# 384-column copies of the first batch and pair 4's casts moved to VectorE, the gate half decoded later

## The chip, the cores and the metric

The kernel runs on one core of a Trainium2 chip. The metric is device time in microseconds for one execution of the whole program, as the median of several runs. TensorE is called PE here, VectorE DVE, ScalarE ACT, GpSimd POOL and SyncE SP, as in the profile.

## What is computed

The reference chains three blocks on inputs of four batches of 576 positions and eight heads of 64 columns:

```python
# attention, block-causal mask with blocks of 64
scores = (q @ k.T) / 8 ; scores = where(mask, scores, -1e9)
x = softmax(scores) @ v                      # [4, 576, 512] after joining the heads
# gated unit
h = relu(x @ w_in) ; u, v = h[..., :512], h[..., 512:]
v_n = (v - mean(v)) / sqrt(var(v) + 1e-6)
x = (u * (w_spatial @ v_n + b_spatial)) @ w_out
# feed-forward
xn = (x - mean(x)) / sqrt(var(x) + 1e-6) * g_ln
out = x + relu(xn @ w_ch1) @ w_ch2
```

All of it is float32. Where the values need more accuracy than one fast product gives, an operand is split into a high part (rounded to the fast format, fp32r) and a low part (the rest), and three products are summed (`mm3`, lines 106 to 108).

## The kernel before

The program has an attention stage, in which the first products of the gated unit are already mixed in, then the spatial products and w_out, then the feed-forward. The change concerns the attention stage.

**Units.** Two heads form a pair, four pairs make a batch, 16 pairs in all. Each pair has nine units (`UNITS`, line 231): first the 64 last query rows of both heads (the tail, c = 4), then blocks of 128 query rows, c = 3, 2, 1, 0 for head j = 0 and 1, which need 512, 384, 256 and 128 key columns. The loop over units `u` (line 533) is written in this order: `scores(u)` on PE into PSUM (tag `sc`, three banks); `softmax(u)`, which is a mask and row minimum on DVE (line 296), then the exponential on ACT (line 303); two units later `transposes(u - 2)`, which turns the weights on PE (line 353, tag `tr`, two banks) and copies them from PSUM to the tiles `pH` (c of 2 and more, the tail among them) and `pL` (c of 0 and 1). At fixed units of the next pair follow `weighted`, the product with v (line 404, `pH` as part 1 and `pL` as part 0), `reciprocals` of the row sums (line 310: DVE, a transpose on PE into a `tr` bank, a copy `rr` on ACT, and two trips through HBM) and `store_x` (line 411, on POOL: the product with the reciprocals at line 414, the high part of `xT` at line 60, its low part at line 417).

**Who copies.** In `put` (line 342) a copy goes to DVE (line 345) if c is at least `PLAN["ev0"]` in the first batch, `PLAN["ev1"]` in the others, and else to ACT (line 347). Before, `ev0` is 3 and `ev1` is 2.

**Preparing a pair.** `prepare(p)` (line 198) is stepped one piece a unit while pair p - 1 is scored. Pairs 0 to 3 are packed (`PACKED` is 4): one cast of the queries and keys to the high part (`cp("hi", ...)`), and the low parts on POOL (line 209). From pair 4 on each head has its own half: two casts, and two subtractions on POOL for each (lines 221 and 223). `cp` picks the engine by `PLAN['hi0']` for pairs below 4 (`v`, DVE, line 56) and `PLAN['hi1']` from 4 on (`s`, ACT, line 58). The operand tiles are two, `stack0` and `stack1`, for even and odd pairs.

**Decoding w_in.** The weights come as 64-bit floats and are decoded on the chip by `decode` (line 81): an activation on ACT (line 88), a shift (line 89) and a shift-and-or (line 90) on DVE; `split` then puts the high part (line 101) and the low part (line 102) of `win` on POOL. There are eight pieces of 128x512, first four of the value half of w_in, then four of the gate half. The set `DECODE` (line 532) names the units at which `decode_in` is stepped: unit 1 starts the loads, the next four units decode the value half and the last four the gate half. Loads of later pieces are asked for as pieces are used. Unit 36 is the first of pair 4, unit 45 the first of pair 5.

**Mixed-in products.** From unit 44 on, `fill` hands out pieces of the value tiles (`vps`) and then of the gate units (`ups`), products of `xT` and `win`, between the units.

**What sets the order.** The program is written in this order, but a scheduler that goes by its own timeline puts each engine's instructions in a row of its own. A decode's ACT instruction (line 88) and its first DVE instruction (line 89) are pinned to the program's order (`here`). On an engine the instructions run in their row; across engines they wait for semaphores.

Of the kernel before, what the change touches and what calls it, by code (L numbers as in the profile page):

```python
# [17 lines left out]

PLAN = {'mm': 3, 'sc': 3, 'tr': 2, 'D': 2, 'hi0': 'v', 'hi1': 's', 'klo0': 'g', 'klo1': 'g', 'qlo0': 'g', 'qlo1': 'g', 'xm0': 'g', 'xm1': 'g', 'xh0': 'g', 'xh1': 'g', 'xl0': 'g', 'xl1': 'g', 'dm': 'g', 'dh': 'g', 'ev0': 3, 'ev1': 2, 'rate': 24500.0, 'vrb': 3, 'ds': 2, 'dy': 1, 'raw': 5, 'yn': 2, 'ts': 3, 'ring': 8, 'wt': 2, 'cb': 1, 'hq': 8, 'packed': 4, 'plain': 3, 'pre': 8, 'py': 10, 'pyn': 4, 'dn0': 2, 'dnn': 5, 'vl': 'v', 'pace': 3, 'wd': 7, 'tl0': 'v', 'tl1': 'v', 'xe': 's', 'pt': 6, 'dstart': 8}


def f32(ap):
    return ap.bitcast(F32)


def view(ap, offset, dims):

    return bass.AP(tensor=ap.tensor, offset=ap.offset + offset, ap=[list(ap.ap[0])] + [list(d) for d in dims])  # L30
# [3 lines left out]
def tile_kernel(  # L34
# [14 lines left out]
    def E(k, p=None):  # L49
        k = PLAN[k if p is None else k + ("0" if p < 4 else "1")]  # L50
        return {"v": nc.vector, "g": nc.gpsimd, "s": nc.scalar}[k]

    def cp(k, p, out, src):
        e = PLAN[k if p is None else k + ("0" if p < 4 else "1")]
        if e == "v":
            nc.vector.tensor_copy(out, src)
        elif e == "s":
            nc.scalar.copy(out, src)  # L58
        else:
            nc.gpsimd.tensor_scalar(out, src, 1.0, 0.0, op0=ALU.mult, op1=ALU.add)  # L60
# [66 lines left out]
    at = tc.alloc_tile_pool(name="at", bufs=2, side="right")  # L127
    p_mm = tc.alloc_tile_pool(name="p_mm", bufs=PLAN["mm"], space=PSUM, side="left")
    p_sc = tc.alloc_tile_pool(name="p_sc", bufs=PLAN["sc"], space=PSUM, side="right")
    p_tr = tc.alloc_tile_pool(name="p_tr", bufs=PLAN["tr"], space=PSUM, side="right")  # L130

# [4 lines left out]

    PACKED = PLAN['packed']
    nat = {}
# [31 lines left out]
    def clear(i):  # L170
        nc.gpsimd.memset(f32(qtail[i][:, 0]), 0.0)
        nc.gpsimd.memset(f32(qtail[i][:, 1]), 0.0)
# [25 lines left out]
    def prepare(p):  # L198

        raw, vt = nat.pop(p), vts.pop(p)  # L200
        st, qt = stacks[p % 2], qtail[p % 2]
        ops[p] = (st, qt, vt, raw)
        low, high = slice(0, 64), slice(64, 128)
        if p < PACKED:
            cp("hi", p, st[:, 0, 0:2, :], raw[:, 0])
            yield
            hi = f32(st[:, 0, 0:2, :])
            for i in range(2):
                E("klo",p).tensor_tensor(st[:, 1, i, :], raw[:, 0, i], hi[:, i], op=ALU.subtract)
            yield  # L210
            for j, rows in enumerate((low, high)):
                nc.scalar.copy(qt[rows, :, 0, 64 * j:64 * j + 64], f32(st[rows, :, 0, 512:S]))
                yield
            return
        if p < PACKED + 2:
            clear(p % 2)
            nc.gpsimd.memset(f32(st[high, :, 0, :]), 0.0)
        for j in range(2):
            cp("hi", p, st[:, j, 1:3, :], raw[:, j])
            yield  # L220
            nc.gpsimd.tensor_tensor(st[low, j, 0, :], raw[low, j, 0, :], f32(st[low, j, 1, :]), op=ALU.subtract)  # L221
            yield
            nc.gpsimd.tensor_tensor(st[high, j, 2, :], raw[high, j, 1, :], f32(st[high, j, 2, :]), op=ALU.subtract)
            yield
        nc.scalar.copy(
            view(qt, 0, [[192, 2], [256, 2], [1, 64]]), f32(view(st, 512, [[3 * S, 2], [S, 2], [1, 64]]))
        )
        yield
# [296 lines left out]
    for _ in prepare(0):  # L525
        pass
# [2 lines left out]
    size = [200 + (S if c == 4 else 128 * (c + 1)) for _, c in UNITS]  # L529
    tot = float(sum(size) * NP)  # L530
    D = PLAN['D']
    DECODE = {1, 7, 12, 17, 22, 38, 42, 46, 50}
    for u in range(NS + 8):
        p, i = divmod(u, NU)
        if u < NS:
# [16 lines left out]
        if i == 0:  # L552
            for q in range(2, PACKED) if p == 0 else range(max(p + 2, PACKED), p + 3):
                load(q)
            load_v(p + 2)
            if p + 1 < NPAIR:
                preps[0] = prepare(p + 1)
        if 0 in preps and i >= 1:
            next(preps[0], None)
        if u in DECODE:  # L560
            next(dec, None)
# [597 lines left out]
```

## Time and profile before

| what | us |
|---|---|
| median of 3 runs | 806.71 |
| lowest and highest run | 805.53 and 810.85 |
| the profiled execution | 807.45 |
| its span, first to last instruction | 805.5 |

The times of the runs and the profiled execution are those of the whole execution; the span leaves out 1.95 us around the instructions. All times in views of the trace count from the start of the span. A row of a timeline gives the start, the length, the engine, the line, the operation, its output and input, how many instructions are merged in it, and in brackets the idle time before it with what ended that. A row of waits gives the engine and line that waited, what it waited for, the sum, the number of waits and the longest.

### The profile page before, as it was taken

What the parts mean: (1) busy time and instruction counts of PE and PEld (TensorE: products, weight loads), DVE (VectorE), ACT (ScalarE), POOL (GpSimd) and SP (SyncE); (2) the same over time, 40 slices, a digit from 0 to 9 for tenths busy, and PEclk for the clock granted to TensorE, in tenths of its full rate; (3) what the DMA queues carried; (4) which work ended last, traced back from release to release, by engine and by line L of the source; (5) the groups of instructions that cost most, each with busy time, mean ns of one, the idle gap of its engine ahead of it and who ended that gap; (6) DMA issues with size and microseconds to landing.
All of it is one profiled execution on the core that took longest, in us unless ns stands there. A gap on an engine that the chain in (4) does not pass through costs nothing.

```text
span 805.5 us, 13270 instructions
## 1 busy us (share of the span) xinstructions
PE 781.1 (97%) x4498; PEld 667.3 (83%) x4498; DVE 528.4 (66%) x1193; ACT 419.2 (52%) x1071; POOL 413.8 (51%) x417
## 2 busy tenths in 40 slices
PE   9998999999999999899999999999999999999997
PEld 4666788778878799888888888888899888888986
DVE  5777666674564377776677777897566578645534
ACT  5777676566755454555354554553345454433421
POOL 5598866654543343222275455455545455545431
PEclk9999999999999999999999999999999999999999
DMA  8966445545251579778520333204001003000002
GB/s 245 208 169 175 130 134 152 141 124 168 68 158 51 151 223 284 214 243 272 165 92 0 105 115 96 79 1 157 1 15 39 1 1 123 22 0 1 1 1 78
DMA packets 53687, 88.66 MB, mean 110 GB/s; under 512 B 6770, under 2 KB 17138, under 8 KB 53620
## 3 DMA queue, kind: packets, MB, share of 16 engines
q1 hardware_dynamic: 53620, 87.83, 36.7%
q8 instruction: 35, 0.57, 0.3%
q14 instruction: 32, 0.26, 0.1%
HBM read 68.85 MB, written 18.95 MB: 109 GB/s over the span
## 4 chain that ended last, share of the span: by engine, by line
PE 72%; DVE 11%; DMA 6%; issue 3%; ACT 3%; POOL 3%; SPq 0%; ACTq 0%; DVEq 0%; POOLq 0%
PE hps L938 21%; PE o L106 8%; PE o L108 8%; PE o L107 8%; PE pv L404 5%; PE tr L353 4%; DMA raw<-in_w_ch_dram 3%; PE sc L281 3%; PE ups L106 2%; PE sc L275 2%; DVE pH L345 2%; PE ups L108 2%; PE ups L107 2%; PE vps L108 1%; PE vps L106 1%
## 5 line engine op out<-in xcount | busy, mean ns | idle before, releaser
L102 POOL TENSOR_TENSOR a<-s,a 128x256 fp32r<-128x256 f32 x96 | 78.2, 818 | 92.4 <-ACT a L97 92.4
L107 PE MATMUL o<-w,h 128*128 128x512 f32 x288 | 112.9, 393 | 0.0
L106 PE MATMUL o<-w,h 128*128 128x512 f32 x288 | 107.8, 398 | 1.6 <-ACT h L930 1.6
L944 DVE TENSOR_TENSOR c<-hps,c 128x384 f32<-128x384 f32 x120 | 66.5, 554 | 54.1 <-PE hps L938 52.3
L108 PE MATMUL o<-w,h 128*128 128x512 f32 x288 | 97.7, 398 | 0.3
L303 ACT ACTIVATE p<-p,nm 128x512 f32<-128x512 f32 (+3 forms) x128 | 71.2, 557 | 34.1 <-DVE nm L296 31.0
L296 DVE CUSTOM_DVE_ANT_0 p<-sc,mask 128x512 f32<-128x512 f32 (+3 forms) x128 | 58.9, 479 | 41.7 <-PE sc L281 16.4
L102 POOL TENSOR_TENSOR a<-w,a 128x256 fp32r<-128x256 f32 x72 | 60.7, 846 | 44.9 <-ACT a L97 39.4
L97 ACT CAST a<-s 128x256 fp32r<-128x256 f32 x96 | 38.4, 404 | 83.6 <-PE hps L938 76.5
L345 DVE COPY pH<-tr 128x512 f32<-128x512 f32 (+1 forms) x88 | 49.7, 575 | 26.0 <-PE tr L353 25.3
L106 PEld LDWEIGHTS o<-w,h 128*128 128x128 f32 x288 | 53.7, 187 | 12.3 <-ACT h L930 2.9
L107 PEld LDWEIGHTS o<-w,h 128*128 128x128 f32 x288 | 54.1, 188 | 10.1
L108 PEld LDWEIGHTS o<-w,h 128*128 128x128 f32 x288 | 53.1, 188 | 9.3 <-DVE h L931 1.6
L353 PE MATMUL tr<-idn,p 128*128 128x128 f32 x320 | 56.1, 283 | 4.2 <-DVE pH L345 4.2
L788 POOL TENSOR_TENSOR gt<-gf,gt 128x576 fp32r<-128x576 f32 (+1 forms) x17 | 25.6, 1507 | 61.8 <-ACT gt L787 61.8
L117 POOL TENSOR_TENSOR rs<-rs,nhalf 128x1 f32<-128x1 f32 x36 | 23.0, 639 | 59.2 <-DVE rs L116 54.0
L353 PEld LDWEIGHTS tr<-idn,p 128*128 128x128 f32 x320 | 38.4, 142 | 14.8 <-DVE pH L345 6.7
L88 ACT ACTIVATE dm<-raw 128x256 f32<-128x256 f32 (+1 forms) x72 | 31.9, 462 | 29.9 <-DVE w L90 9.1
L221 POOL TENSOR_TENSOR stack<-qkt,stack 64x576 fp32r<-64x576 f32 x24 | 34.5, 1436 | 25.0 <-ACT stack L58 24.0
L931 DVE SCALAR_TENSOR_TENSOR h<-c,h 128x384 fp32r<-128x384 f32 x72 | 45.4, 650 | 1.5 <-ACT h L930 1.5
L281 PE MATMUL sc<-stack 128*128 128x512 f32 (+3 forms) x192 | 43.7, 341 | 0.8 <-DVE nm L296 0.4
L930 ACT ACTIVATE h<-c 128x384 fp32r<-128x384 f32 x72 | 35.3, 520 | 16.6 <-DVE c L944 16.2
(183 smaller groups left out, 2257.1 us busy)
## 6 DMA issues: line engine op xcount, KB each, us to landing
raw<-in_w_ch_dram SPq DMA_DIRECT2D x64, 256.0 KB
qkt<-in_qk_dram SPq DMA_DIRECT2D x112, 144.0 KB
vt<-in_v_dram SPq DMA_DIRECT2D x16, 320.0 KB
rb<-r_d SPq DMA_DIRECT2D x32, 144.0 KB
u_d<-ur SPq DMA_DIRECT2D x16, 288.0 KB
us<-u_d SPq DMA_DIRECT2D x16, 288.0 KB
y_d<-ys SPq DMA_DIRECT2D x18, 256.0 KB
yr<-y_d SPq DMA_DIRECT2D x18, 256.0 KB
```

The lines of the kernel that those rows point to most:

```text
L102: {"v": nc.vector, "g": nc.gpsimd}[low].tensor_tensor(lo, src, f32(hi), op=ALU.subtract)
L106: MM(out_ps, lhsT=a[0], rhs=b[0], start=first, stop=False)
L107: MM(out_ps, lhsT=a[0], rhs=b[1], start=False, stop=False)
L108: MM(out_ps, lhsT=a[1], rhs=b[0], start=False, stop=last)
L281: MM(s_ps[:, :nn], lhsT=st[:, j, i, q], rhs=st[:, j, 2, 0:nn], start=(i == 0), stop=(i == 1))
L296: nc.vector.tensor_tensor_reduce(pt[:, o:o + n], s_ps[:, :n], m, -0.125, 3e38, ALU.add, ALU.min, nm[:, i:i + 1])
L303: nc.scalar.activation(pt[:, :n], pt[:, :n], AF.Exp, bias=nm[:, 0:1], scale=-1.0, accum_out=sm[:, col:col + 1])
L345: nc.vector.tensor_copy(out, src)
L353: nc.tensor.transpose(tr[:, o:o + 128], pt[:, 128 * kc:128 * kc + 128], idn)
L931: nc.vector.scalar_tensor_tensor(t[:, 1], src, 0.0, f32(t[:, 0]), op0=ALU.max, op1=ALU.subtract)
L938: MM(ps, lhsT=a[x], rhs=b[y], start=not more and kc == 0 and k == 0, stop=kc == KD // 2 - 1 and k == 2, skip_group_check=True,)
L944: nc.vector.tensor_tensor(out, ps, x, op=ALU.add)
```

## The change

Three places change. `ev0` goes from 3 to 2, so in the first batch the copies with c = 2 (384 columns, two in a pair) move from ACT to DVE. In `prepare`, pair 4's two casts take the engine of the first four pairs, DVE, in place of ACT; later pairs stay on ACT. And the four gate pieces of w_in are decoded at units 42, 45, 48 and 51 in place of 38, 42, 46 and 50.

```diff
-PLAN = {..., 'ev0': 3, 'ev1': 2, ...}
+PLAN = {..., 'ev0': 2, 'ev1': 2, ...}
...
         for j in range(2):
-            cp("hi", p, st[:, j, 1:3, :], raw[:, j])
+            cp("hi", 0 if p == PACKED else p, st[:, j, 1:3, :], raw[:, j])
             yield
...
-    DECODE = {1, 7, 12, 17, 22, 38, 42, 46, 50}
+    DECODE = {1, 7, 12, 17, 22, 42, 45, 48, 51}
```

The scheduler then orders the front of the program anew. On DVE, at the end of pair 2's scoring (line 296 is a mask with its row minimum, `pH_551` are pair 2's weights, `tr_545` and `tr_553` its transposed tail), this stood before:

```order
L296 ISA p_607,nm_608<-sc_603,mask_104 128x256
L296 ISA nm_608 128x1
L90 SCALAR_TENSOR_TENSOR dm_477<-dm_477,de_478 128x512
L296 ISA p_623,nm_624<-sc_619,mask_104 128x256
L296 ISA nm_624 128x1
L345 COPY pH_551<-tr_545 128x4x2x64
L345 COPY pH_551<-tr_553 128x2x64
```

and this stands there now:

```order
L90 SCALAR_TENSOR_TENSOR dm_477<-dm_477,de_478 128x512
L296 ISA p_583,nm_584<-sc_579,mask_104 128x384
L296 ISA nm_584 128x1
L296 ISA p_607,nm_608<-sc_603,mask_104 128x256
L296 ISA nm_608 128x1
L56 CAST stack0_95<-qkt_514 128x1152 x2
L296 ISA p_623,nm_624<-sc_619,mask_104 128x256
L296 ISA nm_624 128x1
L345 COPY pH_551<-tr_545 128x4x2x64
L345 COPY pH_551<-tr_553 128x2x64
```

Pair 4's casts have come in between the two 256-column masks, and a decode instruction has moved two masks ahead.

On DVE, behind pair 4's tail (`pH_916` are pair 4's weights, `dm_927` is the first gate piece of w_in), the order before was:

```order
L345 COPY pH_916<-tr_910 128x4x2x64
L345 COPY pH_916<-tr_918 128x2x64
L89 TENSOR_SCALAR de_928<-raw_394 128x512
L90 SCALAR_TENSOR_TENSOR dm_927<-dm_927,de_928 128x512
L345 COPY pH_916<-tr_944 128x4x128
```

and it is now:

```order
L345 COPY pH_916<-tr_910 128x4x2x64
L345 COPY pH_916<-tr_918 128x2x64
L345 COPY pH_916<-tr_935 128x4x128
L296 ISA p_997,nm_998<-sc_994,mask_104 128x128
L296 ISA nm_998 128x1
```

The two decode instructions are gone from this place; the first gate piece is decoded behind the next pair's tail masks.

On ACT, a little earlier (`stack0_95` receives pair 6's casts, `rr_871` is pair 3's copy of reciprocals, `pL_736` pair 3's weights), the order before was:

```order
L303 ACTIVATE p_968,sm_848<-p_968,nm_969 128x256
L58 CAST stack0_95<-qkt_878 128x1152
L318 COPY rr_871<-rps_869 9x128
L58 CAST stack0_95<-qkt_878 128x1152
L347 COPY pL_736<-tr_896 128x128
L303 ACTIVATE p_984,sm_848<-p_984,nm_985 128x256
L88 ACTIVATE dm_994<-raw_484 128x512
```

and it is now:

```order
L303 ACTIVATE p_959,sm_848<-p_959,nm_960 128x256
L58 CAST stack0_95<-qkt_878 128x1152 x2
L318 COPY rr_871<-rps_869 9x128
L347 COPY pL_736<-tr_896 128x128
L303 ACTIVATE p_975,sm_848<-p_975,nm_976 128x256
L88 ACTIVATE dm_985<-raw_394 128x512
L58 COPY xx_822<-pv_921 128x256
```

The copy of the reciprocals has moved behind the second cast, and one decode activation fewer stands in this stretch.

## Rows read from the trace of the kernel before

**Rows 1.** The page: busy time of each engine and share of the span
```profile
PE 781.1 (97%) x4498; PEld 667.3 (83%) x4498; DVE 528.4 (66%) x1193; ACT 419.2 (52%) x1071; POOL 413.8 (51%) x417
```

**Rows 2.** Waits of PE from 0 to 60 us
```profile
PE tr L353 <- DVE pH L345: 1.5, 4, 0.4
```

**Rows 3.** Windows: length, busy of PE, PEld, DVE, ACT, POOL; granted clock, DMA
```profile
60.00:82.00 22.00, 18.75 (x121) 14.13 (x118) 15.02 (x44) 16.06 (x49) 18.92 (x16) 0.92 0.61 160
66.00:68.00 2.00, 1.45 (x10) 0.71 (x9) 1.53 (x3) 2.00 (x6) 1.93 (x2) 0.77 0.01 2
68.00:70.00 2.00, 2.00 (x13) 1.67 (x10) 1.87 (x2) 0.73 (x2) 1.85 (x3) 0.50 0.64 191
```

**Rows 4.** Waits of PE from 60 to 82 us
```profile
PE sc L260 <- DVE nm L296: 0.6, 1, 0.6
PE tr L353 <- DVE pH L345: 0.6, 1, 0.6
PE tr L353 <- ACT pL L347: 0.6, 1, 0.6
PE rps L316 <- ACT pL L347: 0.5, 1, 0.5
PE tr L353 <- ACT rr L318: 0.5, 1, 0.5
```

**Rows 5.** Timeline of PE, near 40, 67 and 80 us
```profile
39.78 0.87 PE L404 MATMUL pv<-pL,vt 128*64 128x256 f32 x8
40.59 1.09 PE L353 MATMUL tr<-idn,p 128*128 128x128 f32 x8
...
67.05 1.55 PE L404 MATMUL pv<-pL,vt 128*64 128x256 f32 x8
68.53 1.97 PE L353 MATMUL tr<-idn,p 128*128 128x128 f32 x8
71.11 0.55 PE L353 MATMUL tr<-idn,p 128*128 128x128 f32 x3 [0.60 <-DVE pH L345]
...
80.57 0.50 PE L108 MATMUL vps<-win,xT 128*128 128x512 f32 x1 [0.21 <-POOL xT L417]
```

**Rows 6.** Timeline of DVE, 67 to 71 us
```profile
67.37 1.27 DVE L89 TENSOR_SCALAR de<-raw 128x512 uint32<-128x512 uint32 x1
68.77 1.68 DVE L90 SCALAR_TENSOR_TENSOR dm<-dm,de 128x512 uint32<-128x512 uint32 x1
70.37 0.68 DVE L345 COPY pH<-tr 128x512 f32<-128x512 f32 x1
```

**Rows 7.** Timeline of ACT, 60 to 67 us
```profile
60.94 0.65 ACT L88 ACTIVATE dm<-raw 128x512 f32<-128x512 f32 x1
...
65.28 0.24 ACT L318 COPY rr<-rps 9x128 f32<-9x128 f32 x1
65.44 1.15 ACT L58 CAST stack<-qkt 128x1152 fp32r<-128x1152 f32 x1
66.49 0.25 ACT L347 COPY pL<-tr 128x128 f32<-128x128 f32 x1
```

**Rows 8.** Groups by line and form, 0 to 200 us: busy, mean ns
```profile
L58 ACT CAST stack<-qkt 128x1152 fp32r<-128x1152 f32 x20 | 22.4, 1142 | 0.0
...
L345 DVE COPY pH<-tr 128x384 f32<-128x384 f32 x16 | 8.7, 547 | 0.1
...
L347 ACT COPY pH<-tr 128x384 f32<-128x384 f32 x8 | 3.7, 465 | 0.0
...
L56 DVE CAST stack<-qkt 128x1152 fp32r<-128x1152 f32 x4 | 3.0, 758 | 4.9 <-DMA qkt<-in_qk_dram 4.3 <-issue 0.5
```

**Rows 9.** Timeline of DVE, 39 to 46 us
```profile
39.38 0.89 DVE L345 COPY pH<-tr 128x512 f32<-128x512 f32 x2 [0.31 <-PE tr L353]
...
45.44 1.36 DVE L300 TENSOR_TENSOR nm<-nm 128x1 f32<-128x1 f32 x1
```

**Rows 10.** Timeline of POOL near 41 us
```profile
40.76 1.28 POOL L102 TENSOR_TENSOR win<-dm,win 128x512 fp32r<-128x512 f32 x1
```

More of the change, by code (lines that the diff above doesn't have):

```diff
@@ L17 @@
 DRAM = bass.MemoryType.DRAM
-PLAN = {'mm': 3, 'sc': 3, 'tr': 2, 'D': 2, 'hi0': 'v', 'hi1': 's', 'klo0': 'g', 'klo1': 'g', 'qlo0': 'g', 'qlo1': 'g', 'xm0': 'g', 'xm1': 'g', 'xh0': 'g', 'xh1': 'g', 'xl0': 'g', 'xl1': 'g', 'dm': 'g', 'dh': 'g', 'ev0': 3, 'ev1': 2, 'rate': 24500.0, 'vrb': 3, 'ds': 2, 'dy': 1, 'raw': 5, 'yn': 2, 'ts': 3, 'ring': 8, 'wt': 2, 'cb': 1, 'hq': 8, 'packed': 4, 'plain': 3, 'pre': 8, 'py': 10, 'pyn': 4, 'dn0': 2, 'dnn': 5, 'vl': 'v', 'pace': 3, 'wd': 7, 'tl0': 'v', 'tl1': 'v', 'xe': 's', 'pt': 6, 'dstart': 8}
+PLAN = {'mm': 3, 'sc': 3, 'tr': 2, 'D': 2, 'hi0': 'v', 'hi1': 's', 'klo0': 'g', 'klo1': 'g', 'qlo0': 'g', 'qlo1': 'g', 'xm0': 'g', 'xm1': 'g', 'xh0': 'g', 'xh1': 'g', 'xl0': 'g', 'xl1': 'g', 'dm': 'g', 'dh': 'g', 'ev0': 2, 'ev1': 2, 'rate': 24500.0, 'vrb': 3, 'ds': 2, 'dy': 1, 'raw': 5, 'yn': 2, 'ts': 3, 'ring': 8, 'wt': 2, 'cb': 1, 'hq': 8, 'packed': 4, 'plain': 3, 'pre': 8, 'py': 10, 'pyn': 4, 'dn0': 2, 'dnn': 5, 'vl': 'v', 'pace': 3, 'wd': 7, 'tl0': 'v', 'tl1': 'v', 'xe': 's', 'pt': 6, 'dstart': 8}
 def f32(ap):
```

## The prediction

> **What bounds the kernel now.** I read the page first. TensorE (PE) is busy 97% of the span [rows 1], so nothing that an idle engine saves counts until PE is shown waiting for it. The diff touches only the attention stage of the first batch and the decoding of the gate half of w_in. Laid beside each other, the orders of the two kernels part at the first of the moved copies, some 17 us into the span, and run alike again by about 170 us. What stands behind that is passed through: a microsecond won or lost in front moves the end by a microsecond. So I split the front by windows and read PE's waits in it. Up to 60 us the largest wait of PE is 1.5 us in four pieces, for VectorE's (DVE's) copies of transposed tiles [rows 2]. From 60 to 82 us, while pairs 4 and 5 are scored, the mean granted clock is 0.92 [rows 3], and five waits there, for DVE and ScalarE (ACT), make 0.6 + 0.6 + 0.6 + 0.5 + 0.5 = 2.8 us [rows 4]. There the clock itself falls: 0.77 from 66 to 68 us and 0.50, the 1.2 GHz level, from 68 to 70 us [rows 3]. Before it fell PE was busy only 1.45 of 2 us in the first of these windows.
>
> What that costs is in PE's timeline: eight weighted-value matmuls take 0.87 us at 39.78 us and 1.55 us at 67.05 us; the eight transposes behind them 1.09 us at 40.59 us and 1.97 us at 68.53 us [rows 5]. The clock thus costs 0.68 + 0.88 = 1.56 us. Together with the waits, some 4.4 us lie loose between 60 and 82 us. That is the size of the prize; 1% of the kernel is 8.1 us, and a change of less than that is about what a measurement of this kernel can't tell from none.
>
> **The change part by part.** *The gate half's decode moves from units 38, 42, 46 and 50 to 42, 45, 48 and 51.* The work is the same, only later. The one at unit 38 is what matters. On DVE its two instructions stand right between the tail copies and the 512-column copies of pair 4, which PE's next transposes need. They took 1.27 us at 67.37 us and 1.68 us at 68.77 us, and the copy behind them began at 70.37 us [rows 6]; PE then waited 0.60 us for that copy at 71.11 us [rows 5]. In the changed order this place is empty of decoding. PE's eight transposes ended late themselves because of the clock, so the copy can't come more than these 0.6 us earlier to any use: I take 0.6 us (0 if the transposes are the later end, 0.6 at most).
>
> On ACT the same decode's activation (0.65 us at 60.94 us) goes from the front of a stretch without a gap [rows 7]. But the order changes there too: before, the reciprocals' copy at 65.28 us stood between the two casts of pair 6, and now it stands behind both. It frees the PSUM bank that PE's tail transposes wait for (the 0.5 us on `rr` in [rows 4]). So it comes 1.15 us later by the cast and 0.65 us earlier by the activation that is gone, 0.5 us late in all; the small copy behind it (66.49 us), for which PE waits 0.6 us, comes 0.65 us earlier. The tail transposes end at about 66.6 instead of 66.8 us, and the chain in front of them, where PE waited for DVE and ACT too, shortens by up to 0.65 us. Together 0.4 us, between -0.2 and 0.7 us.
>
> The third piece is the last decode pieces on GpSimd (POOL). Now the last xT product of pair 3 is queued ahead of two of them; PE waited 0.21 us for it at 80.57 us [rows 5]: 0.2 us. The decode is due before the first gate product, and in the new order the last one is still some pairs ahead of it; a wait there costs nothing that I can see.
>
> If PE waits less in front of 67 us, the clock may stay up. The waits that go there are 0.4 of some 2 us, so this is far from sure: of the 1.56 us I take half, 0.8 us (0 to 1.56). The gains are 0.6 + 0.4 + 0.2 + 0.8 = 2.0 us.
>
> *Pair 4's casts go from ACT to DVE.* Two casts of 1152 columns take 1.14 us each on ACT and 0.76 us each on DVE [rows 8]. ACT gives off 2.3 us, DVE takes on 1.5 us. On DVE they land between the two 256-column masks of pair 2, in front of its tail copies. Those copies began at 39.38 us and took 0.89 us [rows 9]; PE took the eight transposes that need their banks at 40.59 us without a wait [rows 5], so there was 0.3 us of slack. The casts can begin only when PE has read the old stack for the last time, some 38.8 us; with 1.5 us of casts, a mask and the copies, the first bank is free at about 41.35 us: PE loses about 0.75 us. That is the lower end. Small DVE operations have taken far longer beside a busy POOL: the minimum of one column at 45.44 us took 1.36 us [rows 9], and POOL's own subtraction for the weights takes 1.28 us at 40.76 us [rows 10] and stands, in the new order, right where the casts start. If a cast waits for one such instruction, PE loses 0.75 + 1.28 = 2.0 us; if both do, 3.3 us. I take the middle of the first two, 1.4 us.
>
> The Trainium skill has a rule against this part: on the page "SBUF — State Buffer", section "SBUF: two separate sides", it says that VectorE in a two-port mode and GpSimd hold a shared pair of ports for a whole instruction, and that the other is blocked. The 1.36 us for one column agrees with it. By the rule alone the cast would be late by what is left of POOL's instruction, and the loss would be about 2.0 us where I take 1.4; the sum would come out 0.6 us higher.
>
> *Eight copies of 384 columns (two in each of pairs 0 to 3) go from ACT to DVE.* They take 0.55 us on DVE and 0.47 us on ACT [rows 8]. DVE takes on 8 x 0.55 = 4.4 us, ACT gives off 3.7 us. They stand among the masks of the next pair's tail; they delay the next softmax by up to 0.9 us a pair, and PE at that point has a run of weighted values to do. I take 0.3 us in all (from -1 us, since ACT and the banks come free earlier, to 4.4 us, all of it on the path).
>
> The losses are 1.4 + 0.3 = 1.7 us, the sum is -2.0 + 1.7 = -0.3 us. Against the profiled execution (807.45 us, its span is 805.5 us) that gives 807.15 us. That execution lies 0.74 us above the median of the runs, 806.71 us; so the median of the changed kernel should be about 806.4 us.
>
> **The rivals.** *The whole hiccup goes.* All of the 2.8 us of waits and 1.56 us of clock between 60 and 82 us disappear, and the casts cost the lower 0.75 us: -4.4 - 0.2 + 0.75, about -3.9 us, and the median is 802.8 us. For it: ACT loses work, and the clock fell only after a stretch of waits. Against it: the casts of pairs 5 and 6 are still on ACT, in the same place.
>
> *The stall only moves.* The reciprocals' copy behind two casts takes the place of the decode, the clock falls as before, and DVE's gain of 0.6 us is all there is; the casts cost 0.75 us and the copies nothing. That makes 0.15 us more: 806.9 us. The two casts in a row on ACT speak for it.
>
> *Slower: DVE blocks PE near 39 us.* Both casts wait behind POOL, 3.3 us, and PE, which has just its eight weighted-value matmuls to do, idles long enough that the clock falls as it did at 66 us; the same work as there then costs the same 1.56 us. With the gains without the clock, 1.2 us, and 0.3 us for the copies: 3.3 + 1.56 + 0.3 - 1.2 = 4.0 us, and the median is 810.7 us. It decides from the point where the casts end later than about 41.5 us. For it speaks POOL's busy queue there; against it, that the decode's weights were handled one mask earlier in the new order, so that POOL may be done sooner.
>
> **How the numbers follow.** My forecast 0.45, the whole hiccup 0.2, the moved stall 0.2, slower by DVE 0.15. The first three lie between 802.8 and 806.9 us and the fourth at 810.7 us; with the full 4.4 us of the copies on the path another 4 us would come on top, with the copies' early end 1.3 us off. The range of 801 to 811.5 us takes in the four cases and about 1 us of scatter and leaves these outer mixtures out. For more than 1% faster (below 798.6 us) nearly all PE waits from 12 to 82 us would have to go: 0.04. For more than 1% slower (above 814.8 us) the copies must join the slower rival: 0.05. Same: 0.91.
>
> **What would show it.** Right: no DVE decode between the tail copies and the 512-column copies of pair 4; PE's wait for that copy below 0.2 us; granted clock between 60 and 82 us above 0.92; DVE casts of pair 4 at about 39 to 41 us, at 0.8 us or with a POOL instruction beside them, and PE's transposes behind them 0.7 to 2 us late. Wrong: PE's waits from 12 to 60 us grow by over 3 us (the copies are on the path), or a low clock near 40 us (the slower rival), or all PE waits of 60 to 82 us gone (the first rival), or stretches behind 170 us that differ by more than scatter.

## The result, and the profile after

The changed kernel took 816.17 us (median of 4 executions, 814.84 to 817.99) beside 806.89 us for the kernel before. Its ratio to before is 1.0108, with a 95% interval of 1.0068 to 1.0149. It is slower by about 1%, 9 us, where the prediction said 806.4 us and a range that ended at 811.5.

The profiled execution took 817.99 us, its span is 816.2 us. On the page, the row that answers to [rows 1]:

```profile
PE 788.2 (97%) x4498; PEld 672.2 (82%) x4498; DVE 535.3 (66%) x1203; ACT 415.4 (51%) x1061; POOL 414.7 (51%) x417
```

DVE took on 6.9 us and ACT gave off 3.8 us, in the direction that the change says (the prediction's own figures make it 5.9 and 6.0); PE is busy 7.1 us longer with the same 4498 matmuls. Matmuls that take longer without being more point to the clock. This execution is the slowest of the four and its mean granted clock, 0.989, the lowest; the other three have 0.993 and 0.994, so it shows more of the clock than they do. Windows of the changed kernel, columns as in [rows 3]:

```profile
20.00:30.00 10.00, 9.31 (x62) 6.29 (x61) 5.35 (x19) 7.59 (x24) 4.67 (x4) 0.84 0.78 178
50.00:52.00 2.00, 0.42 (x2) 0.29 (x2) 0.70 (x2) 1.06 (x4) 1.85 (x3) 0.67 0.05 21
52.00:54.00 2.00, 2.00 (x10) 0.92 (x10) 2.00 (x6) 1.70 (x4) 2.00 (x4) 0.50 0.34 85
50.00:60.00 10.00, 8.22 (x41) 4.96 (x41) 4.66 (x15) 6.35 (x21) 7.56 (x9) 0.66 0.47 122
60.00:82.00 22.00, 18.96 (x116) 14.13 (x116) 13.18 (x42) 14.76 (x41) 15.83 (x12) 0.84 0.42 116
100.00:110.00 10.00, 8.64 (x52) 5.97 (x52) 10.00 (x26) 3.91 (x12) 7.23 (x8) 1.00 0.48 118
```

In the kernel before the clock fell once in the front, near 68 us. Now it falls three times: between 20 and 30 us, from 50 us (0.50, the 1.2 GHz level, from 52 to 54 us), and between 70 and 80 us. PE's waits, first from 0 to 60 us (they answer to [rows 2]), then from 60 to 82 us ([rows 4]):

```profile
PE tr L353 <- ACT pL L347: 2.4, 2, 1.8
...
PE sc L275 <- DVE nm L296: 1.1, 3, 0.5
PE tr L353 <- DVE pH L345: 1.1, 3, 0.4
```

```profile
PE tr L353 <- ACT rr L318: 1.7, 1, 1.7
PE sc L260 <- DVE nm L296: 0.6, 1, 0.6
PE tr L353 <- DVE pH L345: 0.3, 1, 0.3
...
```

The wait for DVE that stood first in [rows 2] has shrunk (1.5 to 1.1 us). The two new long waits, 1.8 us for `pL` and 1.7 us for `rr`, are both for small copies on ACT, the engine that was to gain.

Where the time went is read from PE's weighted-value products (L404), whose order is the same in both kernels. The one of pair 1's `pH` begins 2.55 us later than before, pair 2's `pH` 5.93, its `pL` 7.94, pair 3's `pL` 9.25, pair 5's `pL` 12.51; from 126 us on the difference stands between 13.5 and 13.7 us up to 265 us. Of this, 2.9 us come back by the end; PE's waits for `yn` and `gf` behind 300 us are 2.1 and 1.4 us before, 1.2 and 0.7 us here. In the second profile of the changed kernel (run 9) only 0.5 us come back, and in the profiles of the other runs this part of the program gives between +0.4 and -3.6 us, so it is scatter and is not put down to the change. The front decides, as the prediction had it, and its largest single step lies between 42 and 61 us (5.4 us). The timeline of PE, ACT and POOL there:

```profile
51.58 0.69 PE L353 MATMUL tr<-idn,p 128*128 128x128 f32 x2 [1.79 <-ACT pL L347]
52.20 4.32 PE L404 MATMUL pv<-pH,vt 128*64 128x320 f32 x20
```

```profile
45.80 0.40 ACT L303 ACTIVATE p<-p,nm 128x128 f32<-128x128 f32 x1 [1.45 <-DVE nm L296]
...
50.47 0.41 ACT L225 CAST qtail<-stack 128x256 fp32r<-128x256 f32 x1 [4.17 <-POOL stack L221]
50.78 0.40 ACT L303 ACTIVATE p<-p,nm 128x128 f32<-128x128 f32 x1
...
51.17 0.35 ACT L347 COPY pL<-tr 128x256 f32<-128x256 f32 x1
```

```profile
35.68 1.42 POOL L414 TENSOR_TENSOR xx<-xx,rb 128x576 f32<-128x576 f32 x1 [2.60 <-DMA rb<-r_d]
...
45.44 1.41 POOL L221 TENSOR_TENSOR stack<-qkt,stack 64x576 fp32r<-64x576 f32 x1
...
48.48 1.95 POOL L221 TENSOR_TENSOR stack<-qkt,stack 64x576 fp32r<-64x576 f32 x1
```

This is to be read from the bottom up. POOL works without a gap from 35.68 us until past 52 us, and its second L221 ends at 50.43 us. ACT's next instruction, the cast of pair 4's query tail (`qtail`, L225), needs that result and waits 4.17 us. Behind it in ACT's row stand pair 2's last exponential, whose minimum DVE had written by 47.4 us, and the `pL` copy. PE waits 1.79 us for this copy, the clock is then at half, and twenty products that take 2.28 us at full clock take 4.32 us. In the kernel before the same instruction stood behind the next pair's first exponentials and waited for nothing, and the same twenty products ran at full clock:

```profile
46.27 2.28 PE L404 MATMUL pv<-pH,vt 128*64 128x320 f32 x20
```

```profile
48.58 0.39 ACT L225 CAST qtail<-stack 128x256 fp32r<-128x256 f32 x1
```

PE was 2.6 us late at pair 1's `pL` product and 3.4 us late just ahead of this wait; the wait and the slow products bring it to 7.9 us. So 4.5 us of the step arise here, in this execution. Run 9's profile below is of another execution of the same kernel, in which PE does not wait here at all.

The second place is the one that the prediction spoke of, pair 6's casts on ACT:

```profile
72.64 2.21 ACT L58 CAST stack<-qkt 128x1152 fp32r<-128x1152 f32 x2
74.74 0.25 ACT L318 COPY rr<-rps 9x128 f32<-9x128 f32 x1
74.90 0.25 ACT L347 COPY pL<-tr 128x128 f32<-128x128 f32 x1
```

```profile
75.04 1.33 PE L353 MATMUL tr<-idn,tail 128*128 128x128 f32 x5 [1.68 <-ACT rr L318]
76.30 1.54 PE L404 MATMUL pv<-pL,vt 128*64 128x256 f32 x8
```

Both copies that PE needs stand behind both casts. Before, `rr` ran between the casts ([rows 7]) and PE waited 0.5 us for it; now 1.68 us, and the products run at half clock as in [rows 5].

The last rows are DVE's: pair 4's casts (they answer to [rows 9, 10]), and the later decode, near 102 us:

```profile
40.71 2.41 DVE L56 CAST stack<-qkt 128x1152 fp32r<-128x1152 f32 x2 [0.61 <-POOL win L102]
...
101.18 1.46 DVE L90 SCALAR_TENSOR_TENSOR dm<-dm,de 128x512 uint32<-128x512 uint32 x1
...
103.97 1.53 DVE L89 TENSOR_SCALAR de<-raw 128x512 uint32<-128x512 uint32 x1
```

The two casts take 2.41 us where [rows 8] made it 1.5. PE's eight transposes behind them begin at 44.11 us; in [rows 5] they began at 40.59 us. From 100 to 110 us DVE is busy 10.00 of 10 us, with two decode instructions among the value tiles' statistics.

### The profile page after: what moved, and what is told of

Its sections match the earlier page's. It is cut to its first block, busy times and chain, and to the rows that moved or that the text cites. A ratio compares the mean times of both kernels' runs of the same rounds, so it can differ in the third digit from the quotient of the medians.

```text
span 816.2 us, 13276 instructions
## 1 busy us (share of the span) xinstructions
PE 788.2 (97%) x4498; PEld 672.2 (82%) x4498; DVE 535.3 (66%) x1203; ACT 415.4 (51%) x1061; POOL 414.7 (51%) x417
## 4 chain that ended last, share of the span: by engine, by line
PE 72%; DVE 9%; DMA 6%; POOL 5%; issue 4%; ACT 2%; SPq 1%; POOLq 0%; DVEq 0%; ACTq 0%
PE hps L938 21%; PE o L106 8%; PE o L108 8%; PE o L107 8%; PE pv L404 4%; PE tr L353 3%; DMA raw<-in_w_ch_dram 2%; PE sc L281 2%; PE ups L106 2%; PE ups L108 2%; PE ups L107 2%; PE vps L106 2%; DMA vn<-vn_d 1%; DVE pH L345 1%; PE vps L107 1%
## 5 line engine op out<-in xcount | busy, mean ns | idle before, releaser
L345 DVE COPY pH<-tr 128x512 f32<-128x512 f32 (+1 forms) x96 | 54.0, 572 | 33.2 <-PE tr L353 32.7
L107 PEld LDWEIGHTS o<-w,h 128*128 128x128 f32 x288 | 54.1, 188 | 10.1
L221 POOL TENSOR_TENSOR stack<-qkt,stack 64x576 fp32r<-64x576 f32 x24 | 34.7, 1446 | 30.1 <-ACT stack L58 29.4
L414 POOL TENSOR_TENSOR xx<-xx,rb 128x576 f32<-128x576 f32 x16 | 22.7, 1420 | 45.7 <-DMA rb<-r_d 44.2
```

Source lines behind the costliest of these rows:

```text
L107: MM(out_ps, lhsT=a[0], rhs=b[1], start=False, stop=False)
```

## The experiments

There were sixteen runs, each of several executions beside the kernel before (its median was 806.15 to 806.55 us in the four groups). Clock is the mean over the executions of each one's granted clock. A median of 12 executions that lie some 8 us apart is good to about 2 us, so smaller differences between two rows are not shown by themselves. By the clock column, the lower clock of the changed kernel can account for at most some 3 us of the 9 (an estimate: 0.007 of 816 us against 0.004 of 806 us, both rounded).

| kernel | median us | ratio to before, 95% | clock |
|---|---|---|---|
| before | 806.4 (120 executions) | | 0.996 |
| changed | 816.17 | 1.0068 to 1.0149 | 0.993 |
| 1: changed, `qtail` late | 810.71 | 1.0013 to 1.0065 | 0.994 |
| 2: copies alone | 811.93 | 1.0044 to 1.0088 | 0.993 |
| 3: casts alone | 812.00 | 1.0033 to 1.0081 | 0.994 |
| 4: decode alone | 808.27 | 0.9996 to 1.0052 | 0.997 |
| 5: copies and casts | 811.19 | 1.0031 to 1.0089 | 0.992 |
| 6: before, ACT casts behind `rr`, `pL` | 805.68 | 0.9970 to 1.0005 | 0.997 |
| 7: decode, the same rule | 805.88 | 0.9977 to 1.0016 | 0.999 |
| 8: changed, `qtail` late, the same rule | 808.46 | 1.0001 to 1.0048 | 0.998 |
| 9: changed, again | 815.15 | 1.0070 to 1.0149 | 0.993 |
| 10: copies, pair 3's cast back | 812.68 | 1.0050 to 1.0105 | 0.994 |
| 11: as 8, DVE casts behind the mask | 811.53 | 1.0039 to 1.0095 | 0.995 |
| 12: as 6, first decode pieces later | 807.46 | 0.9995 to 1.0031 | 0.996 |
| 13: copies, ACT's orders right | 807.46 | 0.9984 to 1.0045 | 0.996 |
| 14: casts, the rule of 6 | 807.97 | 0.9989 to 1.0047 | 0.995 |
| 15: copies of pairs 0 and 1 | 809.44 | 1.0004 to 1.0063 | 0.995 |
| 16: copies of pairs 2 and 3 | 809.48 | 1.0004 to 1.0067 | 0.993 |

An order that the scheduler chooses is changed by one added ordering edge, without a semaphore: `behind(a, b)` below means that `a` may not stand ahead of `b` in its engine's row.

**1. The query-tail cast late.**

```diff
+        if p == PACKED: behind(qc, exps[3 * NU + 1])   # qc: the copy of line 225
```

> The changed kernel with one thing undone: pair 4's cast of the query tail (L225, on ACT) may not stand ahead of pair 3's first 512-column exponential in ACT's row. Theory 1 (this cast was put into ACT's row ahead of the POOL work that it needs, and holds back pair 2's last exponential and its pL copies, and the clock falls behind that): PE's 1.8 us wait for ACT's pL copy near 51 us is below 0.4 us, the clock between 50 and 60 us is back above 0.85, and the time falls by 4 to 6 us, to 810 to 812 us. Theory 2 (the two casts on DVE, 2.4 us beside POOL, are what PE pays for): at most 2 us less, 814 to 816 us. Theory 3 (the eight 384-column copies on DVE) and theory 4 (the gate half decoded later): no change beyond 1 us, 815 to 817 us.

Measured 810.71 us, 5.5 us less than the changed kernel and 4.4 us less than run 9, the same kernel again. The two kernels' intervals just don't overlap. Waits of PE from 0 to 60 us, and the window of 50 to 60 us:

```profile
PE tr L353 <- DVE pH L345: 2.4, 5, 1.0
...
PE sc L275 <- DVE nm L296: 1.1, 3, 0.5
PE sc L256 <- DVE nm L296: 0.9, 1, 0.9
...
PE tr L353 <- ACT pL L347: 0.6, 1, 0.6
```

```profile
50.00:60.00 10.00, 8.69 (x68) 6.48 (x65) 6.40 (x23) 8.72 (x25) 9.71 (x11) 1.00 0.47 120
```

The 1.8 us wait is gone and the clock stays at 1.00, as theory 1 said. But the waits for DVE shown here make 4.4 us (in the changed kernel 1.1 + 1.1 us above and 0.3 us for the tail's minimum), and the clock still falls between 60 and 82 us (0.84): 4 us remain.

Nor are the 5.5 us shown to be the price of this one place. From pair 1's `pL` product to pair 3's `pH` product run 1 still loses 2.4 us on the kernel before, against 5.4 us in the changed kernel's profile and 2.8 us in run 9's. Two other stretches differ as much. From 20 to 33 us, ahead of all that the added edge moves, the rows of DVE, ACT and POOL are the same in both kernels; yet there the clock fell in the changed kernel, in run 9 too, and stayed at 1.00 in run 1, which loses 0.9 us where they lose 2.4 and 2.2. Pair 0's `pL` products, in the changed kernel and then in run 1:

```profile
27.64 1.55 PE L404 MATMUL pv<-pL,vt 128*64 128x256 f32 x8
```

```profile
26.88 0.87 PE L404 MATMUL pv<-pL,vt 128*64 128x256 f32 x8
```

And behind the edge the scheduler orders anew: the rows of ACT and DVE differ in several places from about 60 and 68 us on, and from 82 to 126 us run 1 loses 1.3 us, the two profiles of the changed kernel 4.4 and 4.5 us.

**2, 3, 4. Each part alone.** The diffs are the three hunks of the change.

> Only the eight 384-column copies of the first batch go to DVE; casts and decode as in the kernel before. In ACT's row the query-tail cast of pair 4 then stands behind both of pair 2's last exponentials but ahead of the pL copies. Theory 1: the pL copies are late by some 2 us, the clock falls in part, 809 to 811 us. Theory 3: the larger part of the loss is here, 812 to 816 us, with PE's waits for DVE between 17 and 36 us grown by over 2 us. Theories 2 and 4: within 1 us of the kernel before, 806 to 808 us.

> Only pair 4's two casts go from ACT to DVE. In ACT's row the query-tail cast then stands behind pair 3's tail exponential and ahead of its second 512-column one, one place earlier than before. Theory 1: a wait of ACT there costs PE under 1.5 us, 806 to 808.5 us. Theory 2: the 2.4 us of casts push the copies for PE and the clock falls near 42 us, 810 to 812 us. Theories 3 and 4: as before, 806 to 807.5 us.

> Only the gate half's decode moves to units 42, 45, 48 and 51. Theory 4 (later decoding meets the value tiles' own work on DVE, ACT and POOL between 84 and 122 us): 810 to 812 us, with the loss between 84 and 122 us. Theories 1 to 3: the clean part of the change, between 805 and 807.5 us, since one decode goes from between pair 4's copies (0.6 us) and the reciprocals come behind two casts (1.3 us in the changed kernel).

Measured 811.93, 812.00 and 808.27 us. Copies and casts each cost over 5 us alone, so the parts add up to 12.6 us (over 806.55 us) where the whole costs 9: they are not additive. For the copies theory 3's number fits within 0.1 us and theory 1's is 1 us short; but the sign that theory 3 named is missing, since PE's waits for DVE from 17 to 36 us grew by 0.3 us only. For the casts theory 2's number fits, but not its picture: the clock stays at 1.00 from 36 to 54 us and falls near 72 us. The decode alone lies between theory 4 and the others, and not clearly above the kernel before. Its trace is the most telling of the three. PE's waits and windows from 60 to 82 us and from 100 to 110 us:

```profile
PE rps L316 <- ACT pL L347: 0.6, 1, 0.6
PE vps L106 <- POOL xT L60: 0.5, 1, 0.5
```

```profile
PE tr L353 <- ACT rr L318: 1.0, 1, 1.0
...
```

```profile
60.00:82.00 22.00, 20.27 (x142) 15.41 (x142) 16.54 (x55) 17.81 (x56) 19.32 (x16) 1.00 0.71 182
100.00:110.00 10.00, 8.36 (x44) 6.38 (x43) 6.33 (x16) 6.09 (x16) 6.08 (x7) 0.83 0.27 80
```

In this order `rr` and `pL` stood ahead of pair 6's casts, and of the hiccup of [rows 4] one wait of 0.6 us was left: from pair 0's first product to pair 4's at 74 us PE gained 4.0 us on the kernel before. Two pairs later `rr` stood behind both casts of pair 8 and PE waited 1.0 us for it; with three more waits of 0.6 us each ahead of it, for DVE and ACT, and the clock, which fell at 106 us, 4.4 us were lost again between 95 and 107 us. That gave theory 5: it matters whether the two long ACT casts stand ahead of the short copies that PE waits for.

**5. Copies and casts, the decode as before.**

> Copies and casts as in the changed kernel, the decode as before. Pair 4's query-tail cast stands in ACT's row between pair 2's two last exponentials, as in the changed kernel. Theory 1 (that place costs 5 to 6 us): 813 to 817 us, with PE waiting over 1.5 us for a pL copy near 51 us. Theory 4 (the later decode is what costs most in the changed kernel): 812.5 us or less.

Measured 811.19 us: theory 4's side, though the trace shows the same `pL` wait of 1.8 us as the changed kernel. So the later decode is part of the loss beside the other two: it adds some 4 to 5 us (816.17 and 815.15 against 811.19), against 1.7 us alone. The intervals overlap in part; the means over the changed kernel's ten executions and run 5's eight are 815.5 and 811.5 us. Between pair 4's `pL` product (at 82 us in the kernel before) and pair 7's `pH` product (126 us) the changed kernel falls back by 4.4 us more, in its second profile (run 9) by 4.5, and run 5 by 0.2. PE's waits in this stretch, 0.3 + 0.2 us in the kernel before, make 3.8 us in the changed one, 2.6 of them for DVE:

```profile
PE tr L353 <- DVE mv L114: 1.0, 1, 1.0
PE sc L281 <- DVE nm L296: 0.9, 1, 0.9
PE tr L353 <- DVE pH L345: 0.7, 2, 0.3
...
```

DVE is full there in both profiles (10.00 of 10 us from 100 to 110 us, in run 9 from 95 to 105 us). The profiles of all runs agree: the eight with the later decode (the changed kernel's two, runs 1, 4, 7, 8, 11 and 12) lose 1.3 to 5.3 us in this stretch, the nine without it -0.2 to 1.1 us.

**6, 7, 8. The ACT casts behind `rr` and the last `pL`.**

```diff
-            cp("hi", p, st[:, j, 1:3, :], raw[:, j])
+            cc = cp("hi", p, st[:, j, 1:3, :], raw[:, j])
+            if p > PACKED: behind(cc, rr[p - 3]); behind(cc, last_pL[p - 3])
```

> The kernel before, with one rule added: from pair 5 on, the two casts on ACT stand behind the reciprocals' copy (L318) and the last pL copy (L347) of three pairs earlier, which PE waits for at a pair's end. Theory 5 (long casts ahead of these short copies in ACT's row cost PE two or three waits in a row, and the clock falls behind them; this is the hiccup of 60 to 82 us): the clock from 60 to 82 us is back above 0.97, and the time falls by 2 to 4 us, to 802.5 to 804.5 us. Theory 6 (the clock falls for other reasons, or the wait moves to the next chain): within 1 us of the kernel before, 805.5 to 807.5 us.

> The later decode alone, with the same rule. In the run of the later decode alone the clock stayed up from 60 to 82 us (rr came ahead of the casts there) and fell at 106 us, behind a 1.0 us wait for rr that stood behind two casts. Theory 5: this fall goes too, 803 to 805.5 us, faster than the kernel before by 1 to 3.5 us. Theory 6: 807 to 809 us, as without the rule.

> The changed kernel with the query-tail cast put back (as in the first run) and the rule on the casts. Theory 5: the 1.7 us wait for rr near 70 us and the fall behind it go, 3 us less than the first run, 806.5 to 809 us. Theory 6: 809.5 to 812 us.

Measured 805.68, 805.88 and 808.46 us. Added to the decode alone the rule takes 2.4 us off, which ends 0.4 us above theory 5's range, and brings the mean clock to 0.999; added to run 1 it takes 2.2 us off, within the range, though in run 8's profile the clock still fell once (0.92 from 60 to 82 us). Both are nearer to theory 5 than to theory 6, each within the scatter. Added to the kernel before it does what it says to the clock and hardly anything to the time. PE's waits from 60 to 82 us in run 6, and two windows:

```profile
PE tr L353 <- DVE pH L345: 2.0, 1, 2.0
PE rps L316 <- DVE nm L296: 1.2, 1, 1.2
```

```profile
60.00:82.00 22.00, 17.54 (x125) 13.36 (x120) 16.90 (x44) 16.37 (x48) 20.21 (x17) 1.00 0.65 171
68.00:70.00 2.00, 0.56 (x5) 0.56 (x6) 2.00 (x5) 0.97 (x4) 1.92 (x2) 1.00 0.94 331
```

The waits for `rr` and `pL` are gone, the clock is 1.00, and now PE waits 2.0 us for the copy behind the decode of [rows 6], which in the kernel before cost only 0.6 us because PE came late itself. Here theory 6 is right: the wait moved. Neither run 6 nor run 7 is shown to be faster than the kernel before; their intervals hold 1.

**9. The changed kernel again.**

> The changed kernel itself, unaltered, to have more than four executions of it beside the others. All theories rest on its 816.2 us: expected 814.5 to 817.5 us. Were it below 813 us, the price of the query-tail cast (5.5 us by the first run) would be smaller.

Measured 815.15 us, with 809.91 to 820.76 over 6 executions. Here `qtail` waited only 2.36 us, because `rb`, on which POOL's row waits, landed sooner: L414 began 8.9 us behind `rr` and not 10.1. At this place PE waited for nothing:

```profile
48.17 0.41 ACT L225 CAST qtail<-stack 128x256 fp32r<-128x256 f32 x1 [2.36 <-POOL stack L221]
```

```profile
49.45 0.59 PE L353 MATMUL tr<-idn,p 128*128 128x128 f32 x2
49.97 3.76 PE L404 MATMUL pv<-pH,vt 128*64 128x320 f32 x20
```

The clock fell all the same, to 0.85 from 50 to 60 us, and the twenty products took 3.76 us. Run 5 shows the reverse: the wait of 1.8 us for `pL`, and a clock of 1.00 from 50 to 60 us. The price of this place thus differs from one execution to the next, from nothing to 1.8 us of waiting, and that the clock falls because of this wait is not shown.

**10, 11. The DVE casts behind the second mask.** In the copies alone, pair 3's cast had come ahead of pair 1's second 256-column mask on DVE; in the changed kernel pair 4's too.

```diff
+            if 2 <= p <= PACKED: behind(cc, mask[(p - 2) * NU + 6])   # on DVE
```

> The copies alone, as in the second run, with one instruction put back: pair 3's cast on DVE (L56) stands behind pair 1's second 256-column mask, as in the kernel before, and not ahead of it. Theory 7 (the copies cost little on DVE; what costs is that this cast, which waits until PE has read the old stack, came ahead of the mask that PE's next chain needs, and the clock fell behind that): 2 to 3.5 us less than the second run, 808.5 to 810 us, with the clock from 20 to 30 us at 1.00. Theory 3 (the eight copies' own time on DVE): within 1 us of the second run, 811 to 813 us.

> The changed kernel with all three orders put right: the query-tail cast late (first run), the ACT casts behind rr and pL (as in the runs six to eight), and the DVE casts of pairs 3 and 4 behind the second 256-column mask. Theory 7: 1.5 to 3 us less than the eighth run, 805.5 to 807 us, no more than the kernel before by 1 us. Theory 3 and 2 (the moved work itself): 808 to 809.5 us.

Measured 812.68 and 811.53 us: no gain in the first, and 3 us more than run 8 in the second. Theory 7 fell. (The clock from 20 to 30 us was 1.00 in run 10, as it said, but so it was in runs 1, 8 and 13, where the cast stands as in the changed kernel.) In run 11 the casts now hold up the copies instead of the mask:

```profile
39.14 2.50 DVE L56 CAST stack<-qkt 128x1152 fp32r<-128x1152 f32 x2
41.57 0.88 DVE L345 COPY pH<-tr 128x512 f32<-128x512 f32 x2
```

```profile
42.30 1.09 PE L353 MATMUL tr<-idn,p 128*128 128x128 f32 x8 [1.37 <-DVE pH L345]
```

This is the wait that the prediction worked out for the casts; ahead of the mask or behind it, 2.5 us in DVE's row are waited for.

**12. Only the first decode pieces later**, at units 42, 44, 46 and 50, with the rule of run 6.

> The kernel before with the rule on the ACT casts (as in the sixth run) and of the decode only the first two pieces later (units 42, 44, 46 and 50 in place of 38, 42, 46 and 50). Theory 4 (the later three pieces meet the value tiles' work from 93 us on, some 2 us): 803 to 804.8 us, better than both the sixth and the seventh run. If the place of the pieces doesn't matter: 805 to 806.5 us.

Measured 807.46 us, no better than runs 6 and 7. By 74 us PE had gained 3.6 us; behind that it waited 1.3 and 1.1 us for POOL's `xT`. Theory 4's finer form isn't borne out.

**13, 14. Copies alone and casts alone, with ACT's orders right.** Run 13 has the edges of runs 1 and 6 (the rule from pair 4 on), run 14 the rule of run 6.

> The copies alone, with both orders of ACT put right: pair 4's query-tail cast behind pair 3's first 512-column exponential, and ACT's casts from pair 4 on behind rr and the last pL copy of three pairs earlier. Theory 5 with theory 1 (order, not own time): 806.5 to 808.5 us, at least 3.5 us less than the copies alone (811.9 and 812.7 us). Theory 3 (own time on DVE): 810.5 to 812.5 us.

> Pair 4's casts alone on DVE, with ACT's casts from pair 5 on behind rr and pL. By the profile of the casts alone PE waits 1.2 us for the copies behind them and 1.2 us for a pL copy behind, some 2 us in all, and the clock falls later, at 70 us, where two ACT casts surround rr. Theory 5: without that fall 807 to 808.5 us, which is the casts' own price, 1.3 to 2.5 us over the sixth run. If the casts cost 5 us by themselves: 810 to 812 us.

Measured 807.46 and 807.97 us, both as theory 5 said: 4.5 and 4.0 us less than runs 2 and 3. Against run 6, the copies cost 1.8 us and the casts 2.3 us by themselves; these two differences are themselves near the scatter. The medians fit theory 5; the traces don't show that the gain arises where it says. By 33 us, ahead of all that run 13's edges move, run 2's profile has lost 2.3 us and run 13's 0.9, with the clock from 20 to 30 us at 0.85 and 1.00; and up to 126 us run 14's profile loses 2.8 us, no less than run 3's 2.1.

**15, 16. The copies of two pairs each.**

```diff
-            if c >= PLAN["ev1" if u >= NU * NP else "ev0"] and ...
+            if c >= (2 if u < 2 * NU or u >= NU * NP else 3) and ...   # run 16: 2 if u >= 2 * NU else 3
```

> Only the four 384-column copies of pairs 0 and 1 go to DVE. By the profiles of the copies alone the loss arises between 20 and 46 us, so nearly all of it should be here: 810 to 812 us. If it comes from pair 4's query-tail cast and the ACT casts of pair 6 (60 us and later): 806.5 to 808.5 us.

> Only the four 384-column copies of pairs 2 and 3 go to DVE. ACT's row ahead of pair 2's last exponentials is then as before; the query-tail cast of pair 4 stands between two pL copies, and both casts of pair 6 ahead of rr. If the loss arises in pairs 0 and 1: 806.5 to 808.5 us. Theory 1 with theory 5 (query-tail cast and ACT casts are enough): 809.5 to 812 us.

Measured 809.44 and 809.48 us: about 3 us each, so the loss is not in one place. Run 15 has the fall of the clock between 20 and 30 us (0.84). Run 16 is untouched up to 58 us and loses behind 60 us, where both casts of pair 6 stand ahead of `rr` and PE waits 1.7 us for it. Run 16 fits theory 5. Run 15 loses some 4 us between 20 and 40 us, where no long cast on ACT stands ahead of a copy; pair 3's cast on DVE stands ahead of a mask there, and putting that back gained nothing in run 10. What run 15 loses is not explained.

## Why the prediction was wrong

PE's weighted-value products (L404) give the account by stretches, in microseconds lost on the kernel before. The times are those of the kernel before, the columns the prediction's terms and the two profiles of the changed kernel:

| stretch | forecast | changed | run 9 |
|---|---|---|---|
| start to pair 0's `pH`, 20 us | 0 | 0.17 | -0.37 |
| to pair 1's `pH`, 33 us | copies 0.3 (all four pairs) | 2.38 | 2.23 |
| to pair 3's `pH`, 58 us (`qtail` lies here) | casts 1.4 | 5.39 | 2.87 |
| to pair 4's `pL`, 82 us | decode and clock -2.0 | 1.26 | 0.69 |
| to pair 7's `pH`, 126 us | 0 | 4.37 | 4.47 |
| to 265 us | 0 | 0.08 | -0.11 |
| to the end | 0 | -2.94 | -0.52 |
| sum | -0.3 | 10.7 | 9.3 |

**What held.** The front decides, and what is lost there is passed through up to 265 us. The decode is gone from between pair 4's copies: the 512-column copy runs at 78.93 us right behind the transposes, and PE waits 0.3 us at most for `pH` in that stretch. No wait for POOL's `xT` is left between 60 and 126 us. PE's transposes behind pair 4's casts came 1.0 us later than pair 1's `pH` product had already been late (1.2 in run 9), within the 0.7 to 2 us that were named.

**The step that failed first: the new place of the decode was put at nothing.** The prediction asked only whether the gate pieces would be decoded in time for their product, found them early enough, and wrote "a wait there costs nothing that I can see". It did not ask what else DVE does at the new place. From 82 to 126 us DVE has the value tiles' statistics beside the masks and copies that PE waits for; with the decode among them it is full, PE's waits grow from 0.5 to 3.8 us, and 4.4 and 4.5 us are lost, the largest loss that both profiles share. Run 5, with the decode as before, loses 0.2 us there, and its median is 4 to 5 us lower. In the decode alone (run 4) the same move gains 4.0 us by 74 us, which is the first rival's size (4.4 us), and by 126 us more than that is lost again.

**The second: the gains of 2.0 us up to 82 us, on ACT and by the clock.** They came out as losses of 1.3 and 0.7 us. The prediction saw `rr` go behind both casts and made it 0.5 us late, because an activation ahead had gone. But this stretch of ACT's row began with a wait of 1.13 us for DVE, and counted from PE's `pH` product of pair 3 `rr` came 1.5 us late. What counts is when PE asks: it was ready at 73.36 us, 0.7 us into the two casts of 2.2 us. It waited 1.68 us in place of 0.5, and the clock fell as before, so the 0.8 us of clock were not gained either. The rival "the stall only moves" was the right picture here and too cheap; by the medians of runs 7 and 8 such an order costs some 2.3 us, within the scatter. The 0.6 us on DVE could not be had beside the rest. Run 6 shows what this wait is: a second one behind the first, 2.0 us once the first is gone.

**The third: an instruction that the prediction did not name.** On ACT it named two, `dm` and `rr`. A third had moved, `qtail` of pair 4, to a place between pair 2's two last exponentials. It took no time in the sum and so had no price. The instruction is short; its price is its input, which POOL delivers at 50.4 us, together with all that stands behind it in ACT's row. The Trainium skill states on the page "PSUM — Partial Sum Buffer", section "Engine vs sequencer instructions", that ScalarE's, VectorE's and GpSimd's queues are strictly first in, first out; the trace agrees, with 4.17 us in which ACT did nothing while the next exponential's input had been there for 3 of them. In one profile this place cost PE 1.8 us of waiting and 2.0 us of half clock, in the other (run 9) no wait. Run 1, which puts it back, is 5.5 us faster by the medians, but by its trace only 0.4 to 3.0 us of that arise here.

**The casts (1.4 us, 0.75 to 3.3) were sized right, the copies (0.3 us, -1 to 4.4) too low but within their bounds.** With ACT's orders changed by edges the casts cost 2.3 us and the copies 1.8 us. Alone, both cost over 5 us, outside both bounds; what brings them from 2 to 5 us is not shown stretch by stretch (runs 13 and 14). The copies' 0.3 us stands against 2.4 and 2.2 us by pair 1's `pH` product alone, 0.9 us where the clock did not fall (run 1). The Trainium skill's rule on the shared ports (page "SBUF — State Buffer", section "SBUF: two separate sides"), by which the casts would have cost 2.0 us, is nearer to run 14's 2.3 us than the 1.4 that was taken; the 1.0 and 1.2 us read behind the casts are nearer to the 1.4, and the scatter decides for neither. The casts' mean rose to 1.2 us beside POOL, from 0.76.

**The slower rival** (DVE blocks PE near 39 us, then the clock falls) was not what happened: PE lost 1.0 and 1.2 us by the transposes behind the casts, not 3.3, and the clock was at 1.00 from 36 to 44 us.

What stays open: why the clock falls in one execution and not in another with the same rows, which makes 1.3 to 1.5 us from 20 to 33 us alone; how the 9 us divide between the copies, the casts and the decode, since the parts are not additive (run 5); and why DVE's casts have no good place in run 11.

## What to carry to other kernels

When work is put off because its result has time, ask what its engine does at the new place and who waits for that: here the later decode fell among DVE's work for PE and cost over 4 us. When a scheduler reorders an engine that runs its row in order, look at every instruction that changed its place there, however short, and ask of each when its input is ready and who stands behind it: here 0.4 us of casting held ACT for 4.2 us in one execution and 2.4 us in another, and PE for 1.8 us and for nothing. A wait that looks small may be one behind another: before pricing its removal, ask what PE would wait for if it came on time. And before a difference between two kernels is put down to a cause, set two profiles of the same kernel side by side: here they differ by 2.5 us in one stretch.

## What had not been expected of the hardware

The clock does not follow one wait. In run 6 PE was busy 0.56 of 2 us from 68 to 70 us and the granted clock stayed at 1.00; in the kernel before it was busy 1.45 of 2 us from 66 to 68 us and the clock fell to 0.77 [rows 3]. Nor does the same row bring the same clock: from 20 to 30 us it was 0.84 in the changed kernel and 1.00 in run 1.

The start of the program differs by 4 us between executions of the same order. In the profiled execution of the kernel before and in that of run 4, the first row of PE's scores is this:

```profile
5.14 1.41 PE L250 MATMUL sc<-qkt 64*64 64x256 f32 x4
```

```profile
5.13 2.18 PE L250 MATMUL sc<-qkt 64*64 64x256 f32 x4
```

In the second the matmuls stay slow until 14 us, while the windows give a granted clock of 1.00 for the first 20 us of both. That 1.00 is no measurement of the start: the trace's record of the clock begins at 5.6 us in the first and only at 14.0 us in the second. All that follows is 4 us later; where two traces are compared here, such a start is taken off first.

The reciprocals' trip through HBM, from the start of `rr` to the start of POOL's product with `rb`, took 8.0 us in the kernel before (24.71 to 32.75), 10.1 us in the changed one (25.61 to 35.68) and 8.9 us in its second profile (25.07 to 33.98). In the changed kernel POOL's row runs from there without a gap until past 52 us.
